# Attention and a feed-forward block woven on one core: two banks of scores per exponential, h in two PSUM banks, and statistics and output scaling shared out anew

## The chip, the cores and the metric

The kernel runs as one program on one core of one Trainium2 chip. The metric is device time in microseconds (us), the median of several executions, as the chip measures them; smaller is better.

## What is computed

Two stages, the second fed by the first. The attention stage takes q, k, v of 4 batches, 8 heads, 768 tokens and 64 features, and 16 centroids for each head. Each query and each key belongs to the centroid that it is most alike to, and a query attends only to keys of its own cluster:

```python
q_assign = np.argmax(np.einsum('bhsd,hcd->bhsc', q_n, c_n), axis=-1)   # k_assign alike
mask = q_assign[:, :, :, None] == k_assign[:, :, None, :]
scores = np.where(mask, scale * np.matmul(q, k.transpose(0, 1, 3, 2)), -1e9)
attn = softmax(scores)                       # maximum subtracted, as usual
x = np.matmul(attn, v)                       # turned to 3072 tokens of 512
h = x @ w_in                                 # 512 -> 1024
solu = h * softmax(h)
mu, var = mean(solu), mean((solu - mu) ** 2)
out = ((solu - mu) / np.sqrt(var + 1e-06) * g_ln) @ w_out     # 1024 -> 512
```

q_n, k_n and c_n are q, k and the centroids over their norms. The output is 3072 rows of 512 in float32.

## The kernel before, in words

**Order.** The kernel records each operation with a name, an engine and what it needs (the class Weave, `add`). Five tables, one for each engine (SP, POOL, PE, DVE, ACT), then say in which order that engine takes the kinds of operation: `S2 V h3` means two of the next banks of scores, one group of value products, three parts of h. A table AWAY gives single operations to another engine. The program is emitted in that order, so each engine's queue is written out by hand; waits between engines follow from the tiles.

**Attention.** The units are pairs of heads (16 in all: 4 batches by 4 pairs). For each pair, q and k are loaded (`ld`), turned by PE (`tp`, line 402, into the tile hreg), copied out (`xa`, 409; `xt` is a turn by VectorE), and multiplied by the normalised centroids (`cl`, lines 471 and 476, into a PSUM tile csc). VectorE turns the product back (`tb`), takes the maximum over centroids (`mx`), makes one-hot rows (`oh`) and turns them (`ot`); `pl` places them beside the features in the tiles qk, so that one matmul of 80 rows gives the score plus a bonus where the clusters agree. The first pair goes in halves (query or key of one head at a time), so that scores start early.

Scores (`S`, line 637) are made for 128 keys by 512 queries, one PSUM bank of 512 float32 per step: 288 banks. ScalarE takes each with one exponential (`E`, 643, tiles `e`, a ring of nine), whose scale and bias make scores without the bonus vanish. The value products (`V`, 660: six matmuls over the key tiles, 192 groups) collect six heads' outputs in one bank (ops), VectorE divides by the sum that a column of ones yields (`N`, lines 672 and 685, into x), and a DMA turns x (`tx`).

**Feed-forward.** The tokens come in 24 blocks of 128, f = 0 to 23. For each, `h` is made in four parts (746; f2 is the half of 512 columns, each half two parts of two matmuls), then: VectorE's maximum over 1024 (`hm`, 752), ScalarE's exponential with its sum (`ex`, 758, into e_sb), VectorE's product u = e * h (`u`, 765, which reads h out of PSUM a last time), a DMA transpose of u (`tu`; for the last two blocks PE does it, `ptu`, with copies out, 742), VectorE's statistics of u (`bn`, 776, two of 512; `ag`, 780) for the variance, three small steps on POOL for alpha, the factor of the row (`at`, `al`, 786 to 795), four parts of `y` (810) against the centred w_out, scaling by alpha (`sc`, 825 on ScalarE or 827 on VectorE) and the output's DMA (`ou`, 837). The work of block f lies between the scores of later units; the last three blocks end alone.

**PSUM**, eight banks: three single banks for scores (tiles sps, pool ps_s), three for h (the tile hreg), one for the value products (ps_o), one for clustering products and y (ps_m). Block f takes banks 0 and 1 of hreg where f is even, 2 and 1 where it is odd (`at` and `both`, with the halves' order changed), so one of its two halves needs only u of block f-2, and the other u of block f-1.

**Start.** The centroids are loaded (c_all), VectorE and POOL work out the inverse norm (877 to 889) and scale them (890), PE turns the result (899), VectorE masks it into blocks (903), and only then can the first clustering product run. A column sum of w_out (`su`, `me`, `ce`) centres it. Matmuls without use (`wm`, `fl`, line 854, tile idle_p) keep PE busy through the start.

Of the kernel before, what the change touches and what calls it, by code (L numbers as in the profile page):

```python
# [22 lines left out]
class Weave:  # L23
# [6 lines left out]
        ld4 lv si ld6 lv ld lg lv ld2 lo2 lv lo ld2 lo ld6 li4 tx ld lv ld6 lv tx lv tu ld5 lv ld tx  # L30
        ld tu ld tu ld8 ou ld tu ou ld4 lv ld7 lv ld tu ld4 ou tx ld tu ld4 ou tx ld5 ou ld tu ld2
        lv ld tu ld tx ld4 ou ld3 ou pl ld5 tu lv ld4 lv tu ou tu ld3 lv ou tx ld lv tu ld2 pl ou tx
        ld2 ou pl tu ou lv tx tu pl ou tu2 tx2 tu ou tx2 tu ou tu ou tx tu ou tu ou tu ou6
    """
    ORDER["POOL"] = """
        zo po =ca0.0.0.1.0 ca =pl0.0.0.1.1 pl cv =ca0.1.0.1 =ca0.1.0.0 =pl0.0.1.0.0 pl z
        =pl0.0.1.0.1 ca pl ca =cv0.1.1 =ca0.2.1.1 pl =ca0.2.0.1 pl2 ca2 =ca0.3.1.1 cv =pl0.2.0.0
        =ca0.3.1.0 cv pl =ca0.3.0.1 z pl =cv0.3.1 =ca1.0.0.0 cv =ca1.0.1.0 pl =z4 gs z ca =pl1.0.1.1
        sg ca =pl1.0.0.1 pl2 wi4 =ca1.1.1.0 =cv1.0.1 =ca1.1.0.1 cv =ca1.1.1.1 =at1 =ca1.2.0.1 at ca
        al =pl1.1.1.1 cv =pl1.1.0.0 pl bl pl ca z =ca1.2.1.1 al at ca cv =pl1.2.1.1 =pl1.2.0.0 al  # L40
        =pl1.2.0.1 pl =ca2.0.1.0 bl cv =ca1.3.0.1 at =cv1.3.1 =ca1.3.1.0 ca al =pl1.3.1.1 =pl1.3.0.0
        pl cv bl pl =cv2.1.0 ca =pl2.0.0.0 pl =at5 pl2 at al =ca2.0.1.1 =ca2.1.0.0 =pl2.1.0.1
        =ca2.1.1.1 ca cv al =ca2.3.0.0 bl cv =pl2.1.1.1 =ca2.2.0.1 =ca2.1.1.0 =pl2.1.0.0 =ca2.2.0.0
        pl bl =ca2.3.1.1 at2 al =ca2.2.1.0 cv ca cv pl =ca2.3.1.0 pl at pl =pl2.3.1.1 =pl2.3.1.0 ca
        pl at pl al =ca3.0.0.0 ca =ca3.0.1.0 bl ca =cv2.3.1 al =ca3.1.1.1 cv =pl3.0.0.0 =pl3.0.1.1
        pl bl =ca3.2.0.1 al ca =cv3.0.1 cv pl at2 ca al =pl3.1.1.1 =ca3.3.0.0 =ca3.2.0.0 =cv3.1.1
        =pl3.2.0.1 al =pl3.1.0.1 pl =ca3.2.1.0 =cv3.2.1 pl =ca3.3.0.1 cv ca cv at =ca3.3.1.0 pl cv
        al ca at =pl3.3.0.1 at =pl3.3.1.1 al pl ca =at17 at al2 at al at al =at21 at al2 =at22 at
        al3 at al
    """  # L50
    ORDER["PE"] = """
        wm fl2 tp fl2 tp fl8 cp tp fl7 cl tp fl11 cl fl16 tp S tp S cq S2 tp S tp2 S V S tp V S tp
        cl V S tp2 S V S2 V tp S V S gt tp S2 cl S2 V2 S V S tp S V S V S tp S V S cl S2 V S V3 S2
        tp2 S V S V2 S tp S V S2 cl S V S V2 S2 V S su S3 V4 S3 su S V S2 V S V2 S2 me S2 V2 S2 V2
        S2 cl S2 V S V S V2 h S3 h S h S h S V S V3 S2 h V h V S2 V S h S V S h S2 V S V h S V h S3
        V3 y2 S y S h2 S h V y S2 V2 S h cl V S2 h V h S3 h S V y S y3 V S2 V S V h V S h S V S V S
        y S h y S3 V y S V S V2 S y S V2 S2 cl h V S h S2 h V S V S2 y V S V2 S2 y S2 y2 S V h V S V
        S2 V2 S V cl S2 V2 S cl S V2 S2 y S V S V S y S V S y S V S2 y S V S V2 h V S h S h2 S y4 S
        V S h2 S V S h2 S V S V cl V h S h S V S2 cl S h S h V S2 V h S V2 h y2 S2 y2 S2 V2 S h S2 h
        V S V S2 V2 y S V2 S y S3 y h y V3 S V S2 h V S h S V h S2 h V S cl V S2 V S V cl V S2 h V  # L60
        y2 S y S V S y S2 V S V2 h S h S2 V S cl S V S2 y S y3 V2 S V S V S y S2 V y S2 V3 S2 y S y
        V2 S V2 S2 h S h S2 h2 S3 V h V S y S V S2 h V y2 S2 y V S V h S h S V3 S2 cl V h S V2 h S y
        S3 h S h S V2 y V S h y S h S y S V S2 V2 h2 S2 V2 y V y S V S h S h S2 V h2 S V y2 h2 S V2
        S2 V2 S y S2 h S2 h S V2 S V2 y S y S V S h2 S2 h S h S2 V3 S y h V S V2 h S V S h2 S2 y V S
        y S y h y S h V h2 y h V y V y S2 y S2 V h3 y4 h2 V y V y V y2 h2 ptx y4 h2 y3 h2 y ptu2 y8
        ptu2 y4
    """
    ORDER["DVE"] = """
        cn ca cf xa tb mx oh ot =pl0.0.0.0.1 pl tb xa mx xa cb cv oh xa ot xa =xa0.2.0.1 xa ca tb mx
        oh ot N gk =xa0.3.1.0 pl xa tb mx oh xa ot N tb mx cv xa N pl oh xa3 N ot =pl0.3.0.1  # L70
        =pl0.3.0.0 pl N tb mx oh ot N sk xt2 N ce2 N ce2 tb ce mx ce2 N ce hm N ca u xt bn N hm oh
        bn ag ot u N xt hm sc bn u bn2 tb hm ag mx N oh u =bn3.0 bn ot =xt1.3.1 ag bn N hm xt ag cv
        =xt2.0.1 sc N u tb mx bn oh ot xt2 cv N bn sc xt hm N tb mx oh tb N ag ot u mx xt N bn2 ag
        oh ot xt hm N xt u bn2 hm xt tb ag u mx N oh tb bn hm bn ot ag mx u oh sc N bn2 ot hm
        =xt3.0.1 N u bn xt bn N bl =xt3.1.1 xt tb ag hm mx tb oh N xt u bn sc xt ot tb hm ag N
        =mx3.2 sc =oh3.2 N u bn ag =ot3.2 N mx bn oh ot N xt sc hm ca bn ag u bn2 N xt hm bl tb bl u
        bn N ag mx hm bn cv ag oh u ot bn N hm bl u =bn15.0 bn ag hm N sc u N bn3 hm N u bn hm N u N
# [111 lines left out]
def kernel(  # L189
# [11 lines left out]
    nc = tc.nc  # L201
# [1094 lines left out]
```

## Time and profile before

| | us |
|---|---|
| median of 3 executions (226.42 to 226.63) | 226.57 |
| the profiled execution, whole | 227.3 |
| its span on the core | 225.3 |

| what the profile's page says | value |
|---|---|
| granted TensorE clock, mean | 1.00 |
| HBM read, written | 23.11 MB, 6.29 MB |
| chain that ended last, by engine | PE 80%, DVE 10% |
| the same chain, by line | scores (637) 23%, h (746) 16%, y (810) 16%, value products (660) 12% |

The page is of one profiled execution. Busy time is the sum of an engine's instructions; a busy matmul may still be drawn out by waiting. In rows that group instructions the number behind the bar is the sum of busy time, then the mean of one in ns, then the idle time ahead of them with what ended it. In rows of the chain the first number is the time from the span's start, the second the length, and a bracket names a wait. In the rows by stage the columns are named where they are shown. PEld is the loading of weights, which overlaps the matmuls. Tiles go by the program's names.

### The profile page before, as it was taken

To read this page: it belongs to the slowest core of one execution; us is meant where nothing else is said; L and a number is where in the kernel's file an instruction comes from. 1 tells how busy PE (TensorE), PEld (TensorE's weight loads), DVE (VectorE), ACT (ScalarE), POOL (GpSimd) and SP (SyncE) were. 2 spreads that over 40 slices of the span, in tenths; PEclk is the share of its full clock that TensorE was granted. 3 is DMA by queue.
4 is the path that set the end of the run, shared out by engine and by line. 5 is a ranking of instruction groups with operands and counts; after the bars stand their busy time and mean duration, and the time that the engine had idled before them with its cause. 6 is when DMAs were issued, how large, how long until landed. Compare 5 with 4: busy or idle time off the path is not lost.

```text
span 225.3 us, 6745 instructions
## 1 busy us (share of the span) xinstructions
PE 219.2 (97%) x2501; PEld 146.8 (65%) x2501; DVE 200.3 (89%) x359; ACT 191.3 (85%) x366; POOL 127.7 (57%) x246
## 2 busy tenths in 40 slices
PE   8999999999999999999999999999999999999993
PEld 8877864666666767666566656676666677665452
DVE  2799997899999999999999899898998996879982
ACT  3399988999979999998989979899989899964353
POOL 3379985942385597289995670957965102122341
PEclk9999999999999999999999999999999999999999
DMA  5999994289999999799997998789771724659522
GB/s 182 366 370 354 196 243 191 47 163 220 187 179 153 213 179 169 148 161 175 184 219 155 147 215 149 180 170 162 175 166 58 93 28 116 90 155 177 166 83 103
DMA packets 117327, 38.80 MB, mean 172 GB/s; under 512 B 105640, under 2 KB 112816, under 8 KB 117296
## 3 DMA queue, kind: packets, MB, share of 16 engines
q1 hardware_dynamic: 117008, 38.06, 79.0%
q8 instruction: 19, 0.31, 0.6%
q10 hardware_dynamic: 288, 0.33, 0.4%
q14 instruction: 12, 0.10, 0.2%
HBM read 23.11 MB, written 6.29 MB: 130 GB/s over the span
## 4 chain that ended last, share of the span: by engine, by line
PE 80%; DVE 10%; ACT 2%; POOL 2%; issue 2%; DMA 1%; SPq 1%; DVEq 0%; ACTq 0%; POOLq 0%
PE sps L637 23%; PE hreg L746 16%; PE yps L810 16%; PE ops L660 12%; PE hreg L402 3%; PE csc L476 3%; PE idle_p L854 3%; DVE xt L427 2%; ACT e L643 2%; PE csc L471 1%; DMA raw<-in_q_dram 1%; DVE nmax L752 1%; DVE y L827 1%; DVE oh L510 1%; PE hreg L609 1%
## 5 line engine op out<-in xcount | busy, mean ns | idle before, releaser
L643 ACT ACTIVATE e<-sps 128x512 bf16<-128x512 f32 x288 | 150.6, 610 | 10.5 <-PE sps L637 8.6
L637 PE MATMUL sps<-qk 80*128 80x256 bf16 (+3 forms) x648 | 98.9, 260 | 0.3
L637 PEld LDWEIGHTS <-qk 80*128 80x128 bf16 (+1 forms) x648 | 52.1, 97 | 32.0 <-issue 8.6
L660 PEld LDWEIGHTS <-e 128*128 128x128 bf16 x1152 | 52.5, 97 | 16.0 <-issue 4.0
L660 PE MATMUL ops<-v,e 128*128 128x65 bf16 x1152 | 58.7, 193 | 0.5 <-DVE x L685 0.3
L746 PE MATMUL hreg<-w_in_sb,xT 128*128 128x512 bf16 x192 | 54.4, 379 | 0.0
L810 PE MATMUL yps<-w_out_c,uT 128*128 128x512 bf16 x184 | 49.9, 379 | 0.3 <-DVE y L827 0.3
L765 DVE TENSOR_TENSOR u<-e_sb,hreg 128x1024 bf16<-128x1024 bf16 (+1 forms) x25 | 29.1, 1166 | 5.0 <-ACT e_sb L758 4.9
L758 ACT ACTIVATE e_sb<-hreg,nmax 128x1024 bf16<-128x1024 f32 x24 | 26.8, 1118 | 6.7 <-DVE nmax L752 6.5
L776 DVE BATCH_NORM_STATS2 bs<-u 128x6 f32<-128x512 bf16 x48 | 31.6, 676 | 0.3
L550 POOL COPY qk<-oht 32x384 f32<-32x384 f32 x40 | 20.6, 515 | 18.8 <-DVE oht L523 14.9
L752 DVE TENSOR_REDUCE nmax<-hreg 128x1 f32<-128x1024 f32 x24 | 28.9, 1203 | 1.3 <-PE hreg L746 1.1
L456 POOL CAST qk<-xt 64x768 bf16<-64x768 f32 (+1 forms) x31 | 25.5, 823 | 6.9 <-DVE xt L409 3.0
L458 POOL TENSOR_SCALAR qk<-xt 64x768 bf16<-64x768 f32 (+1 forms) x28 | 23.4, 836 | 4.0 <-PE yps L810 2.3
L810 PEld LDWEIGHTS <-uT 128*128 128x128 bf16 x200 | 17.8, 97 | 11.5 <-ACT uT L742 0.8
L746 PEld LDWEIGHTS <-xT 128*128 128x128 bf16 x192 | 16.5, 97 | 8.1 <-issue 0.6
L792 POOL TENSOR_SCALAR esq<-es,mv 128x1 f32<-128x1 f32 x24 | 8.1, 339 | 22.6 <-DVE mv L780 22.0
L427 DVE STREAM_TRANSPOSE xt<-raw 128x768 f32<-128x768 f32 x22 | 20.9, 959 | 0.0
L685 DVE TENSOR_TENSOR x<-ops,den 128x256 bf16<-128x256 f32 (+1 forms) x39 | 18.9, 486 | 1.3
L786 POOL TENSOR_SCALAR es<-esum 128x1 f32<-128x1 f32 x24 | 5.6, 239 | 23.3 <-ACT e_sb L758 14.9
L568 POOL CAST v<-vf 128x384 bf16<-128x384 f32 x27 | 14.3, 532 | 7.7 <-DMA vf<-in_v_dram 4.7
L795 POOL TENSOR_TENSOR alpha<-esq,halves 128x1 f32<-128x1 f32 x24 | 13.4, 560 | 2.0
(82 smaller groups left out, 186.6 us busy)
## 6 DMA issues: line engine op xcount, KB each, us to landing
vf<-in_v_dram SPq DMA_DIRECT2D x16, 384.0 KB, 4.4
out_dram<-y SPq DMA_DIRECT2D x23, 256.0 KB, 2.8
raw<-in_q_dram SPq DMA_DIRECT2D x44, 96.0 KB, 3.2
raw<-in_k_dram SPq DMA_DIRECT2D x44, 96.0 KB, 3.4
w_g<-in_moe_w_out_dram SPq DMA_DIRECT2D x4, 512.0 KB, 8.0
w_st<-in_moe_w_in_dram SPq DMA_DIRECT2D x4, 512.0 KB, 6.9
raw<-in_q_dram SPq DMA_DIRECT2D x4, 384.0 KB, 7.2
raw<-in_k_dram SPq DMA_DIRECT2D x4, 384.0 KB, 7.8
```

The lines of the kernel that those rows point to most:

```text
L427: nc.vector.transpose(xt[:], raws[b, p, i][:].rearrange("p j c -> p (j c)"))
L456: VEC[e].tensor_copy(dst, src)
L458: VEC[e].tensor_scalar(dst, src, scalar1=inv_C, scalar2=1.0, op0=Alu.mult, op1=Alu.mult)
L637: nc.tensor.matmul(sps_[n, k][:, c0:c0 + w], side(b, h // 2, 1, h % 2, keys)[r], side(b, h // 2, 0, h % 2, slice(s0 * P, s0 * P + w))[r])
L643: nc.scalar.activation(es[n, k][:, :w], sps_[n, k][:, :w], Act.Exp, scale=exp_scale, bias=-exp_scale)
L660: nc.tensor.matmul(opss[g][:, s, :VW], es[n, k][:, c0:c0 + P], v1[slot(b, h // 2)][:, h % 2, kt, :VW], start=(kt == 0), stop=(kt == n_t - 1))
L746: uses(nc.tensor.matmul(hreg[:, at(f, f2)[1], :], xTs[f][:, dc, :], w_in_sb[:, dc, f2 * FF2:(f2 + 1) * FF2], start=(dc == 0), stop=(dc == ...
L752: uses(nc.vector.tensor_reduce(ff[f, "nmax"][:], pair_of(f), axis=AXY, op=Alu.max, negate=True), *both(f))
L758: uses(nc.scalar.activation(ff[f, "e"][:], pair_of(f), Act.Exp, bias=ff[f, "nmax"][:], accum_out=ff[f, "esum"][:]), *both(f))
L765: uses(nc.vector.tensor_tensor(ff[f, "u"][:, at_], ff[f, "e"][:, at_], pair_of(f)[:, at_], op=Alu.mult), *banks)
L776: nc.vector.bn_stats(ff[f, "bs"][:, f2, :], ff[f, "u"][:, f2, :])
L810: ins = nc.tensor.matmul(dst, ff[f, "uT"][:, at(f, f2)[0] * (n_fc // 2) + c, :], w_out_c[:, fc, cols], start=(fc == chunks[0]), stop=(fc = ...
```

## The change

**Scores.** The pool of scores holds two tiles of two banks, and one exponential of 1024 elements takes both banks. Scores go into a bank when the exponential of the pair before the last is done (four banks back, where it was three). The ring of exponentials' results is five pairs of tiles.

```diff
+    RING_E = 5
-    ps_s = ctx.enter_context(tc.tile_pool(name="ps_s", bufs=3, space=bass.MemoryType.PSUM))
+    ps_s = ctx.enter_context(tc.tile_pool(name="ps_s", bufs=2, space=bass.MemoryType.PSUM))
 def scores(n, k):
-        sps_[n, k] = ps_s.tile([P, 512], F32, name="sps", tag="sps")
+        at_ = bank_at[n, k]
+        if at_ % 2 == 0:
+            sps_[at_ // 2] = ps_s.tile([P, 2, 512], F32, name="sps", tag="sps")
-    def expo(n, k):
-        es[n, k] = ep.tile([P, 512], BF16, name="e")
-        nc.scalar.activation(es[n, k][:, :w], sps_[n, k][:, :w], Act.Exp, scale=exp_scale,
-                             bias=-exp_scale)
+    def expo(j):
+        e = ep.tile([P, 2, 512], BF16, name="e")
+        pair = BANKS[2 * j:2 * j + 2]
+        for x, bank in enumerate(pair):
+            es[bank] = e[:, x]
+        m = len(pair)
+        nc.scalar.activation(e[:, :m], sps_[j][:, :m], Act.Exp, scale=exp_scale, bias=-exp_scale)
```

**h.** That leaves two banks for hreg. Both halves of a block's h now need u of the block before; block 22 takes its two banks from the pool of scores, and block 23 waits for u of block 21.

```diff
-    hreg = ps_h.tile([P, 3, FF2], F32, name="hreg")
+    hreg = ps_h.tile([P, 2, FF2], F32, name="hreg")
     def at(f, f2):
-        return (f2, f2) if f % 2 == 0 else (1 - f2, 2 - f2)
+        return (f2, f2)
     def pair_of(f):
-        return hreg[:, 0:2, :] if f % 2 == 0 else hreg[:, 1:3, :]
+        return tail["h"] if f == n_f - 2 else hreg[:]
-                    was = f - 1 if f2 else f - 2
-                    if was >= 0:
+                    was = n_f - 3 if f == n_f - 1 else f - 1
+                    if f == n_f - 2:
+                        nd.append(ename(*BANKS[2 * n_e - 4]))
+                    elif was >= 0:
                         nd.append(f"u{was}")
```

**Variance.** In 12 of 24 blocks (the odd ones up to 21, and 22) VectorE's product u also sums its row (a custom instruction, L790, and a read), a small step makes the mean (`nm`), and ScalarE sums the squares of u minus the mean (`sq`, L807, into e_sb, where the block's exponential had been). The exponential of the block after the next waits for that square. POOL's steps for alpha follow suit.

```diff
+    BY_ACT = {*range(1, n_f, 2), n_f - 2} - {n_f - 1}
     def f_u(f, half=None):
+        if f in BY_ACT:
+            h_uses(f, nc.vector.tensor_tensor_reduce(
+                out=ff[f, "u"][:], in0=ff[f, "e"][:], in1=pair_of(f), scale=1.0, scalar=0.0,
+                op0=Alu.mult, op1=Alu.add, accum_out=ff[f, "usum"]), *banks)
+            return
+    def f_mean(f, e):
+        VEC[e].tensor_scalar(ff[f, "nmean"], ff[f, "usum"], scalar1=-1.0 / d_ff, scalar2=None,
+                             op0=Alu.mult)
+
+    def f_var(f):
+        nc.scalar.activation(ff[f, "e"][:], ff[f, "u"][:], Act.Square, bias=ff[f, "nmean"],
+                             accum_out=ff[f, "usq"])
-        nd = ([f"hm{f}"] + ([f"u{f - 2}"] if f >= 2 else []) +
+        nd = ([f"hm{f}"] + ([f"{'sq' if f - 2 in BY_ACT else 'u'}{f - 2}"] if f >= 2 else []) +
```

**Outputs.** ScalarE scales all of them but one half of the last block's; before, VectorE had ten and a half. y of block 21 goes into the bank of the value products.

**Start.** The centroids are loaded twice (c_two, on two queues) and turned by PE as they come; ScalarE copies the result (`ct`). The inverse norm is worked out meanwhile, one matmul spreads it over the partitions (`ci`), and VectorE multiplies the two into the blocks, those of the first pair first (`cg`, then `cf` and `cb`). The first two loads of q go on ScalarE's queue, those of k on SP's. ScalarE takes all four first copies `xa` and one placement `pl`; 18 matmuls without use instead of 26, and 29 of the later ones instead of 46.

```diff
-    nc.vector.tensor_scalar(c_n[:], c_all[:].unsqueeze(1).to_broadcast([P, 2, D]),
-                            scalar1=c_inv[:], scalar2=None, op0=Alu.mult)
     def turn_centroids():
-        nc.tensor.transpose(cs["t"][:].rearrange("p a h c -> p (a h c)"),
-                            c_n[:].rearrange("p a d -> p (a d)"), ident_f[:])
+        cs["t"] = ps_o.tile([P, 2, P], F32, name="cps", tag="ops")
+        nc.tensor.transpose(cs["t"][:, 0, :], c_two[:].rearrange("p a d -> p (a d)"), ident_f[:])
+    def spread_inverse():
+        nc.tensor.matmul(cs["t"][:, 1, :], c_inv[:].to_broadcast([P, P]), ident_f[:])
```

**Tail.** The PE transposes of the last blocks use the two halves of one pair of banks in turn (`tail["a"]`); the copies out of them stay on the engines that had them (one of block 22 on VectorE, the other three on ScalarE, lines 740 and 742 before).

**Order.** All five tables are new. One line of PE's, with h of blocks 17 to 20 (four parts each):

```diff
+        V4 S2 h4 S2 V S2 y2 V2 S2 V S2 h4 S3 V S V3 S2 y V y V2 S h4 V S2 y4 V2 S3 y2 h4 y2 S2 V S V
```

On ScalarE before, between the exponentials of h of two blocks (e_sb out of hreg: first block 15, last block 16) stand six exponentials of one bank of scores:

```order
L758 ACTIVATE e_sb_3944,esum_3943<-hreg_111,nmax_3906 128x1024
L643 ACTIVATE e_3964<-sps_3947 128x512
L643 ACTIVATE e_3974<-sps_3956 128x512
L643 ACTIVATE e_3983<-sps_3967 128x512
L643 ACTIVATE e_3996<-sps_3978 128x512
L643 ACTIVATE e_4004<-sps_3985 128x512
L643 ACTIVATE e_4024<-sps_4009 128x512
L758 ACTIVATE e_sb_4036,esum_4035<-hreg_111,nmax_4022 128x1024
```

On ScalarE after, from the exponential of block 16 to that of block 17, the four of scores take two banks each, one of them stands right behind block 16's own, and one right ahead of block 17's; the scaling of an output is among them:

```order
L779 ACTIVATE e_sb_3617,esum_3616<-hreg_111,nmax_3584 128x1024
L649 ACTIVATE e_3640<-sps_3590 128x1024
L870 ACTIVATE y_3662<-yps_3509,alpha_3470 128x512
L649 ACTIVATE e_3676<-sps_3622 128x1024
L649 ACTIVATE e_3685<-sps_3664 128x1024
L649 ACTIVATE e_3711<-sps_3691 128x1024
L779 ACTIVATE e_sb_3731,esum_3730<-hreg_111,nmax_3698 128x1024
```

Six single banks have become four pairs, and the scaling (L870) has come between.

On VectorE at the start before, the norm of the centroids, their scaling (L890) and, behind the first placing of tokens (L458), the mask of the turned product (L903); cps is the turned product:

```order
L877 ISA c_n_148,c_nsq_149<-c_all_118 128x64
L877 ISA c_nsq_149 128x1
L882 RECIPROCAL c_r0_153<-c_s0_151 128x1
L883 SCALAR_TENSOR_TENSOR c_r0_153<-c_r0_153,c_nsq_149,c_s0_151 128x1
L886 TENSOR_SCALAR c_norm_156<-c_r0_153 128x1
L889 RECIPROCAL c_inv_158<-c_norm_156 128x1
L890 TENSOR_SCALAR c_n_148<-c_all_118,c_inv_158 128x128
L458 TENSOR_SCALAR qk0_99<-xt_211 64x3x128
L903 TENSOR_TENSOR w_out_c_113<-cps_222,own_142 128x256
L409 COPY xt_199<-hreg_111 128x384
L485 STREAM_TRANSPOSE cst_251<-csc_242 128x192
```

On VectorE at the start after, c_two is the raw centroids, c_t their turned copy, cps the spread inverse norm; L956 writes the blocks:

```order
L921 ISA c_sq_146,c_nsq_147<-c_two_118 128x64
L921 ISA c_nsq_147 128x1
L927 RECIPROCAL c_r0_151<-c_s0_149 128x1
L929 TENSOR_SCALAR c_s1_153<-c_s0_149 128x1
L931 SCALAR_TENSOR_TENSOR c_norm_155<-c_r0_151,c_nsq_147,c_s1_153 128x1
L934 RECIPROCAL c_inv_157<-c_norm_155 128x1
L956 TENSOR_TENSOR w_out_c_113<-c_t_159,cps_181 64x2x16 x2
L457 TENSOR_SCALAR qk0_99<-xt_210 64x3x128
L484 STREAM_TRANSPOSE cst_235<-csc_223 128x192
```

The scaling of the centroids is gone, the product for the first pair (L956) stands right behind the inverse norm and ahead of the tokens' step (L457), and the copy out of hreg (L409) has left VectorE.

357 lines of the change are left out of this document (193 added, 164 removed).

## The prediction

> **What bounds the kernel now.** I read the page's first part, then busy time by stage, then the chain of waits, then PE's own waits, and last the timeline at the places that the change touches.
>
> ```profile
> span 225.3 us, 6745 instructions
> PE 219.2 (97%) x2501; PEld 146.8 (65%) x2501; DVE 200.3 (89%) x359; ACT 191.3 (85%) x366; POOL 127.7 (57%) x246
> ```
>
> Three engines are nearly full, so the share of busy time doesn't decide. The stages do. The rows of h give two of their borders: block 0 starts its h at 47.2 and block 12 at 150.8 (block 21 follows at 199.2).
>
> ```profile
> L746 PE MATMUL hreg<-w_in_sb,xT x20: 377/377/382, 47.2 to 57.9; 128*128 128x512 bf16 x20
> ```
> ```profile
> L746 PE MATMUL hreg<-w_in_sb,xT x44: 377/378/383, 150.8 to 179.4; 128*128 128x512 bf16 x44
> ```
> ```profile
> 150.80:199.20 48.40, 48.30 (x570) 32.33 (x568) 42.51 (x70) 45.52 (x88) 19.69 (x40) 1.00 0.67 120
> 47.20:150.80 103.60, 102.85 (x1198) 67.97 (x1195) 98.88 (x169) 96.44 (x185) 67.32 (x122) 1.00 0.94 175
> ```
>
> The columns are length, then busy time of PE, PEld, DVE, ACT, POOL. VectorE is 95% busy in the middle and 88% later. A busy PE may still be a waiting PE, so its pace has to be read. Six adjoining steps of the chain of waits, and one clustering product:
>
> ```profile
> 91.98 0.78 PE csc L476 x8
> ...
> 187.52 0.45 PE sps L637 x8
> 187.97 0.43 PE hreg L746 x2
> 188.41 0.23 PE sps L637 x4
> 188.63 0.43 PE hreg L746 x2
> 189.07 0.45 PE sps L637 x8
> 189.52 0.55 PE ops L660 x18
> ```
>
> Each step starts where the last one ends. So this is PE's bare pace: 0.43 for a part of h (two matmuls of 512 columns, a quarter of a token block's h; y is alike), 0.22 for a bank of scores, 0.18 for a group of six value products. I multiply these by what stands in PE's order from the first scores to the last y (288 banks, 192 value groups, 96 parts of h and 96 of y, 15 full clustering products, some 11 us of transposes and column sums) and get 204. The trace takes 211, from 10.82 (below) to the end of this row:
>
> ```profile
> 220.04 1.97 PE L810 MATMUL hreg<-w_out_c,uT 128*128 128x256 bf16 x16 [0.45 <-ACT uT L742]
> ```
>
> Even if all 7 that are left were waits (part of it is small steps between kinds of work), PE is at its limit, and nothing that lightens another engine can give more than that.
>
> ```profile
> PE idle_p L854 <- DVE halves L858: 1.0, 1, 1.0
> PE hreg L810 <- ACT uT L742: 0.5, 1, 0.5
> PE ops L660 <- DVE x L685: 0.3, 1, 0.3
> PE yps L810 <- DVE y L827: 0.3, 1, 0.3
> ```
>
> PE's listed waits after the start come to about 1. So the change can gain at the start and at the tail, and a little in between; it loses wherever it makes PE wait.
>
> **The change, part by part.** *ScalarE's exponentials.* Twelve one-bank exponentials in a row, and the groups that give the other prices:
>
> ```profile
> 20.09 6.20 ACT L643 ACTIVATE e<-sps 128x512 bf16<-128x512 f32 x12
> ```
> ```profile
> L776 DVE BATCH_NORM_STATS2 bs<-u 128x6 f32<-128x512 bf16 x48 | 31.6, 676 | 0.3
> L780 DVE BATCH_NORM_AGGREGATE mv<-bs 128x2 f32<-128x12 f32 x24 | 4.6, 192 | 0.2
> L825 ACT ACTIVATE y<-yps,alpha 128x512 f32<-128x512 f32 x13 | 9.0, 692 | 5.8 <-PE yps L810 3.2 <-POOL alpha L795 2.5
> L827 DVE TENSOR_SCALAR y<-yps,alpha 128x512 f32<-128x512 f32 x10 | 7.4, 740 | 1.3 <-POOL alpha L795 0.8 <-issue 0.4
> ```
>
> 6.20 over 12 is 0.52, with the last one's end in it, which a next one would overlap: 0.51, two 1.02. No row shows a two-bank exponential of scores. The nearest is the exponential of h, with as many elements out of two banks; here are its rows with its neighbours, one token block from h to u:
>
> ```profile
> 100.56 1.03 PE L746 MATMUL hreg<-w_in_sb,xT 128*128 128x512 bf16 x4
> ...
> 101.63 1.23 DVE L752 TENSOR_REDUCE nmax<-hreg 128x1 f32<-128x1024 f32 x1
> ...
> 102.89 1.11 ACT L758 ACTIVATE e_sb<-hreg,nmax 128x1024 bf16<-128x1024 f32 x1 [0.39 <-DVE nmax L752]
> ...
> 103.90 0.19 ACT L758 ACTIVATION_READ_ACCUMULATOR e_sb<-hreg,nmax 128x1 f32 x1
> 103.99 1.07 ACT L643 ACTIVATE e<-sps 128x512 bf16<-128x512 f32 x2
> ...
> 104.21 1.18 DVE L765 TENSOR_TENSOR u<-e_sb,hreg 128x1024 bf16<-128x1024 bf16 x1
> ```
>
> From its start to the next exponential is 1.10, with the read of the sum in it: bounds 0.91 (1.10 less 0.19) and 1.02 (no gain). I take 0.92, so 144 pairs save 14.4 (0 to 16). ScalarE gets 12 squares with a sum, priced as that row (1.10): +13.2; ten scalings from VectorE at 0.69: +6.9; a few copies at the start: +1.4. It ends at 191.3 - 14.4 + 21.5 = 198, not lower. VectorE loses 24 statistics (15.8), 12 aggregates (2.3) and ten scalings (7.4), gains about 3 for the means and sums (small ones of 0.1 to 0.2): 178. By themselves both cost and gain nothing: PE's work covers them, as above. If ScalarE's cover goes, that is the third rival.
>
> *The scores' ring*: three banks become two pairs. PE's pace gives a pair 204/144 = 1.4 us, ScalarE needs 0.92 for it; with two slots, PE comes back to a slot 2.8 after it began to fill it. A pair is ready 0.65 after its start (0.22 for the first bank, 0.39 until the second is written, as in the row at 10.82 below, and a hop), so its exponential may be about 1.2 late before PE notices; with three single banks the same reckoning gives about 1.1. Priced at nothing (-1 to +2).
>
> *h in two banks.* Now a block's h may begin only after u of the block before has been read out. Before it need not:
>
> ```profile
> 174.88 0.60 PE L746 MATMUL hreg<-w_in_sb,xT 128*128 128x512 bf16 x2
> ```
> ```profile
> 175.19 1.22 DVE L765 TENSOR_TENSOR u<-e_sb,hreg 128x1024 bf16<-128x1024 bf16 x1
> ```
>
> The matmuls for block 16 start in the third bank 0.3 before u of block 15 has even begun. [...]
>
> The loop: the first four matmuls of h 0.86, then from 100.56 to u's end at 105.39 4.83, then about 0.1 to start PE again: 5.8 between the starts of two blocks, with no queue on VectorE or ScalarE. Against it stands PE's own work between those starts in the new order, from block 12 to block 21. For 17 to 18: four parts of h 1.72, eight banks 1.78, four value groups 0.73, two parts of y 0.86: 5.1. All nine: 5.95, 6.63, 5.97, 5.45, 5.46, 5.09, 5.42, 5.96, 5.92, in sum 51.9. The same count for before gives 47.45 where the trace takes 48.40, so I add 2% to each. Where scores stand between h's parts the loop grows with them: 6.0, 7.05 and 6.25 for the first three. The loop is longer than the work by 0.3, 0.2, 0.2, 0.2, 0.6 and 0.3 at six of the nine: +1.8. On top comes the queue: a two-bank exponential stands ahead of the block's own in ScalarE's order. Filled right after h, it runs from 2.4 to 3.3 of the loop, while the maximum is ready at 3.2; so 0.13 at most blocks, 0.1 for the sum that VectorE now reads with u in odd blocks, and more where a pair is late: +1.2 (0 to +3.5). So +3.0 (1.8 to 5.3).
>
> *From block 0 to block 12* the same loop meets intervals of 6 us and more; only the first four are near it. New waits about 1, old ones (some of the 1 above) gone: +0.3 (-1.5 to +3). Scalings now queue behind exponentials on ScalarE and hold the one bank of y longer; that is within the same bounds, since PE's whole wait for it was 0.3. The new order of SP moves outputs and turns among the loads; their longest cover is eight load buffers, and none of PE's waits above names a load: nothing.
>
> *Start.* What leads to the first scores now:
>
> ```profile
> 0.72 0.41 ACTq L384 DMA_DIRECT2D raw<-in_q_dram  x1
> ...
> 4.70 0.16 DVE L889 RECIPROCAL c_inv<-c_norm 128x1 f32<-128x1 f32 x1
> ...
> 4.79 0.85 PE L402 MATMUL hreg<-ident_f,raw 128*128 128x128 f32 x3
> ...
> 5.67 0.48 ACT L409 COPY xt<-hreg 128x384 f32<-128x384 f32 x1 [0.37 <-PE hreg L402]
> ...
> 6.28 0.42 PE L899 MATMUL cps<-ident_f,c_n 128*128 128x128 f32 x1
> ...
> 6.74 0.42 DVE L903 TENSOR_TENSOR w_out_c<-cps,own 128x256 f32<-128x256 f32 x1
> ...
> 7.43 0.16 PEld L471 LDWEIGHTS csc<-xt,w_out_c 128*32 128x32 f32 x8
> ...
> 10.82 0.39 PE L637 MATMUL sps<-qk 80*128 80x256 bf16 x2
> ```
>
> The clustering product at 7.43 waits for the centroids' chain (7.16), not for the tokens (6.15). After the change the raw centroids are transposed early, and the inverse norm (4.86) needs one matmul and two small products, to about 6.1: the product can start at about 6.3. That is -1.1; four placements on three engines instead of two I put at -0.2, and the first q, issued 0.45 later on ScalarE's queue, may give some back: -1.2 (-1.6 to -0.4).
>
> *Tail*: y of block 22 is left to cover the last copies of u, which cost PE 0.5 above; by hand a new wait of 0.3 for the copy on VectorE stands against it: -0.2.
>
> The sum: -1.2 + 3.0 + 0.3 - 0.2 = +1.9. The profiled execution took 227.3 (span 225.3 and 2.0 around it), the median of the runs is 226.57; the difference is carried over to the median: 228.5.
>
> **The rivals.** (1) *The loop fits*: blocks wait only where the bare loop is over the work (+1.8), and all old waits between block 0 and 12 go (-1.5), since VectorE is empty enough to take each maximum at once: 226.57 - 1.2 + 1.8 - 1.5 - 0.5 (the tail's old wait) = 225.2. For it: VectorE falls by 22. Against it: the loop's 5.8 was already taken without a queue. 0.20. (2) *PE isn't the bound, VectorE is*: then time falls with the fullest other engine, from 200 to 198, and by the start: 226.57 - 2.3 - 1.2 = 223.1. For it: 95% in the middle. Against it: the unbroken steps of PE. 0.07. [...] (3) *ScalarE becomes the bound* from block 5 on: between blocks 12 and 21 it has 33 pairs, 9 exponentials of h, 4 squares and 7 scalings, 30.4 + 9.9 + 4.4 + 4.8 = 49.5, against 45.5 before in 48.4. If each of about 30 pairs there is late by a further 0.1, it decides: 228.5 + 3 = 231.5. 0.13. (4) *No change*: start and loop cancel, 226.6. 0.08. That the change doesn't do what it says is ruled out: the order on ScalarE has the 144 exponentials of 128x1024. My forecast has 0.52, between 227.1 and 230.
>
> What a measurement of this kernel can tell from no change is about 0.2%, 0.45 us. Faster is (1) and (2) with a bit of (4): 0.28; same 0.07; slower 0.65. The range, 224.4 to 231.3, leaves out (2) and the upper part of (3).
>
> **What the new profile would show.** Right: first scores at about 9.6; 144 exponentials near 1.0 each; ScalarE at 198, VectorE at 178; h behind u by name among PE's waits, and the nine starts of h from block 12 to 21 taking 55 to 57 where their bare work takes 52.9; PE idle or stretched there, dense elsewhere. Wrong: if those nine take 53 or less, the loop is not a bound and the kernel is faster; if PE's waits name the exponentials of scores all along, it is the third rival; if the first scores stay at 10.8, the start's chain was misread.

## The result and the profile after

The changed kernel takes 232.80 us (median of 4 executions, 232.29 to 234.0), where the one before took 226.57: a ratio of 1.029 (95% interval 1.026 to 1.033; the two medians alone give 1.027). It is slower, as forecast, but by 6.2 us and not by 1.9, and above the range. The profiled execution took 232.29 whole, 5.0 more than that of before (227.3). The other 1.2 is spread between executions: that of after lies 0.5 under its median, that of before 0.7 over it.

The page's first part, after:

```profile
span 229.9 us, 6419 instructions
...
PE 218.6 (95%) x2449; PEld 145.5 (63%) x2477; DVE 181.8 (79%) x339; ACT 200.9 (87%) x259; POOL 125.9 (55%) x243
```

VectorE lost 18 us of work, ScalarE gained 10, and PE does the same in 4.6 us more of span. The chain that ended last, 80% of it on PE before, now runs through the other engines for half of the span:

```profile
PE 45%; ACT 20%; DVE 17%; POOL 8%; issue 6%; DMA 2%; ACTq 0%; DVEq 0%; POOLq 0%
```

The groups of ScalarE's exponentials and squares, and of PE's scores:

```profile
L649 ACT ACTIVATE e<-sps 128x1024 bf16<-128x1024 f32 x144 | 141.1, 1030 | 13.6 <-PE sps L640 12.9
L640 PE MATMUL sps<-qk 80*128 80x256 bf16 (+3 forms) x648 | 92.8, 260 | 3.0 <-ACT e L649 2.1
...
L807 ACT ACTIVATE e_sb<-u,bs 128x1024 bf16<-128x1024 bf16 x12 | 13.9, 1157 | 2.1 <-DVE bs L803 2.1
```

141.1 over 144 is 0.98 for a pair, nearer to two single ones (1.02) than to the 0.92 that I took. Where the time went is read by stage. Four rows of PE give the borders after the change, the first scores and the first h of blocks 0, 12 and 21 (columns: start, length):

```profile
9.53 0.60 PE L640 MATMUL sps<-qk 80*128 80x256 bf16 x4
...
48.61 0.59 PE L767 MATMUL hreg<-w_in_sb,xT 128*128 128x512 bf16 x2
...
153.11 0.81 PE L767 MATMUL hreg<-w_in_sb,xT 128*128 128x512 bf16 x3
...
208.84 0.81 PE L767 MATMUL hreg<-w_in_sb,xT 128*128 128x512 bf16 x3
```

Busy time of the engines between these borders, after (columns as in the prediction: stretch, length, then PE, PEld, DVE, ACT, POOL):

```profile
9.53:48.61 39.08, 36.94 (x470) 26.38 (x471) 35.99 (x72) 33.10 (x37) 28.41 (x48) 1.00 0.88 227
48.61:153.11 104.50, 103.07 (x1180) 68.15 (x1195) 89.85 (x159) 98.60 (x124) 68.45 (x124) 1.00 0.99 176
153.11:208.84 55.73, 53.33 (x616) 35.55 (x623) 39.61 (x69) 51.70 (x69) 20.48 (x45) 1.00 0.57 115
208.84:229.90 21.06, 17.41 (x116) 9.02 (x114) 11.95 (x22) 12.62 (x21) 4.99 (x13) 0.98 0.50 129
```

The two stretches of before that the prediction did not show:

```profile
10.82:47.20 36.38, 35.86 (x472) 25.71 (x472) 33.49 (x69) 33.60 (x67) 28.99 (x47) 1.00 0.80 234
...
199.20:225.30 26.10, 22.32 (x167) 12.10 (x165) 19.83 (x35) 11.92 (x21) 8.02 (x21) 1.00 0.50 130
```

The new order puts other work into a stretch, so from each length I take PE's own work in it, counted with the prediction's prices:

| stretch | length before, after | PE's work before, after | lost by the change | forecast |
|---|---|---|---|---|
| to the first scores | 10.82, 9.53 | | -1.3 | -1.2 |
| to h of block 0 | 36.38, 39.08 | 34.4, 34.3 | +2.8 | 0 |
| to h of block 12 | 103.60, 104.50 | 100.0, 100.3 | +0.6 | +0.3 |
| to h of block 21 | 48.40, 55.73 | 47.45, 51.9 | +2.9 | +3.0 |
| to the end | 26.10, 21.06 | 22.6, 17.6 | 0.0 | -0.2 |

The last column's terms hold but for one: the stretch of 39 us behind the first scores loses 2.8, twice what the start gained. PE's listed waits, after:

```profile
PE sps L640 <- ACT e L649: 2.1, 6, 0.7
...
PE hreg L401 <- DMA raw<-in_q_dram: 0.7, 1, 0.7
PE ops L665 <- DVE x L690: 0.5, 2, 0.3
PE hreg L401 <- DVE xt L408: 0.5, 2, 0.3
...
PE hreg L767 <- DVE bs L803: 0.2, 1, 0.2
```

They name exponentials of scores. The first matmul of h is named only once, behind the small step for the mean (L803) that follows u on VectorE. One loop shows why (ScalarE, VectorE and PE, from h of block 17 to h of block 18):

```profile
185.02 1.89 PE L767 MATMUL hreg<-w_in_sb,xT 128*128 128x512 bf16 x8
...
186.95 1.23 DVE L773 TENSOR_REDUCE nmax<-hreg 128x1 f32<-128x1024 f32 x1 [0.94 <-PE hreg L767]
...
188.38 1.11 ACT L779 ACTIVATE e_sb<-hreg,nmax 128x1024 bf16<-128x1024 f32 x1
...
189.47 2.85 ACT L649 ACTIVATE e<-sps 128x1024 bf16<-128x1024 f32 x3
...
189.71 1.22 DVE L790 CUSTOM_DVE_ANT_0 u<-e_sb,hreg 128x1024 bf16<-128x1024 bf16 x1 [0.93 <-issue]
190.55 0.61 PE L640 MATMUL sps<-qk 80*128 80x128 bf16 x8 [0.68 <-ACT e L649]
...
191.00 1.90 PE L767 MATMUL hreg<-w_in_sb,xT 128*128 128x512 bf16 x8
```

h, maximum, exponential, u and the next h follow each other with gaps of 0.2 or less, 5.98 in all. But the exponential of scores that starts at 189.47 ends at 190.5 too, and frees the pair that PE fills just ahead of h. From the block's exponential two paths lead to the next h, and they end within 0.1 of each other.

### The profile page after: what moved, and what is told of

Same layout as the page of the kernel before. It is cut to its first block, busy times and chain, and to the rows that moved or that the text cites. A ratio compares the mean times of both kernels' runs of the same rounds, so it can differ in the third digit from the quotient of the medians.

```text
span 229.9 us, 6419 instructions
## 1 busy us (share of the span) xinstructions
PE 218.6 (95%) x2449; PEld 145.5 (63%) x2477; DVE 181.8 (79%) x339; ACT 200.9 (87%) x259; POOL 125.9 (55%) x243
## 4 chain that ended last, share of the span: by engine, by line
PE 45%; ACT 20%; DVE 17%; POOL 8%; issue 6%; DMA 2%; ACTq 0%; DVEq 0%; POOLq 0%
ACT e L649 13%; PE sps L640 13%; PE hreg L767 11%; PE yps L855 10%; PE ops L665 5%; ACT e_sb L779 4%; ACT e_sb L807 2%; DVE xt L408 2%; POOL qk L457 2%; POOL qk L455 2%; DVE u L790 2%; DVE cst L484 2%; DVE nmax L773 2%; DMA raw<-in_q_dram 2%; PE hreg L401 1%
## 5 line engine op out<-in xcount | busy, mean ns | idle before, releaser
L649 ACT ACTIVATE e<-sps 128x1024 bf16<-128x1024 f32 x144 | 141.1, 1030 | 13.6 <-PE sps L640 12.9
L640 PE MATMUL sps<-qk 80*128 80x256 bf16 (+3 forms) x648 | 92.8, 260 | 3.0 <-ACT e L649 2.1
L665 PE MATMUL ops<-v,e 128*128 128x65 bf16 x1152 | 56.5, 193 | 1.0 <-DVE x L690 0.5
L855 PE MATMUL yps<-w_out_c,uT 128*128 128x512 bf16 x163 | 45.6, 379 | 1.2 <-DVE uT L759 0.3
L767 PE MATMUL hreg<-w_in_sb,xT 128*128 128x512 bf16 x177 | 45.3, 379 | 0.6 <-DVE bs L803 0.2
L455 POOL CAST qk<-xt 64x768 bf16<-64x768 f32 (+1 forms) x31 | 25.8, 832 | 9.6 <-DVE xt L426 3.4
L855 PEld LDWEIGHTS <-uT 128*128 128x128 bf16 x200 | 17.4, 97 | 11.3 <-ACT uT L761 0.6
L457 POOL TENSOR_SCALAR qk<-xt 64x768 bf16<-64x768 f32 (+1 forms) x28 | 23.0, 822 | 1.2
L837 POOL TENSOR_SCALAR esq<-es,mv 128x1 f32<-128x1 f32 x12 | 4.1, 339 | 26.7 <-DVE mv L817 22.7
L870 ACT ACTIVATE y<-yps,alpha 128x512 f32<-128x512 f32 x23 | 16.0, 694 | 2.8 <-POOL alpha L840 1.7
L794 DVE TENSOR_TENSOR u<-e_sb,hreg 128x1024 bf16<-128x1024 bf16 (+1 forms) x13 | 14.8, 1138 | 3.6 <-ACT e_sb L779 3.2
L790 DVE CUSTOM_DVE_ANT_0 u<-e_sb,hreg 128x1024 bf16<-128x1024 bf16 x11 | 13.4, 1219 | 4.3 <-ACT e_sb L779 3.1
L813 DVE BATCH_NORM_STATS2 bs<-u 128x6 f32<-128x512 bf16 x24 | 16.2, 683 | 0.2
```

The costliest lines, as they stand in the source:

```text
L455: VEC[e].tensor_copy(dst, src)
L457: VEC[e].tensor_scalar(dst, src, scalar1=inv_C, scalar2=1.0, op0=Alu.mult, op1=Alu.mult)
L640: nc.tensor.matmul(sps_[at_ // 2][:, at_ % 2, c0:c0 + w], side(b, h // 2, 1, h % 2, keys)[r], side(b, h // 2, 0, h % 2, slice(s0 * P, s0 * ...
L649: nc.scalar.activation(e[:, :m], sps_[j][:, :m], Act.Exp, scale=exp_scale, bias=-exp_scale)
L665: nc.tensor.matmul(opss[g][:, s, :VW], es[n, k][:, c0:c0 + P], v1[slot(b, h // 2)][:, h % 2, kt, :VW], start=(kt == 0), stop=(kt == n_t - 1))
L767: h_uses(f, nc.tensor.matmul(pair_of(f)[:, f2, :], xTs[f][:, dc, :], w_in_sb[:, dc, f2 * FF2:(f2 + 1) * FF2], start=(dc == 0), stop=(dc == ...
```

## The experiments

Times are medians; ratios are to runs of the kernel before on the same chip. "Loop" is the time from one block's first h to the next one's.

**Is it u's hold on h's banks?** The product is made without h, in all blocks but the last:

```diff
+        other = ff[f, "e"][:] if f < n_f - 1 else pair_of(f)
-                out=ff[f, "u"][:], in0=ff[f, "e"][:], in1=pair_of(f), scale=1.0, scalar=0.0,
+                out=ff[f, "u"][:], in0=ff[f, "e"][:], in1=other, scale=1.0, scalar=0.0,
```

> The changed kernel (232.8), but u is made from e_sb alone (e times e, except in the last block), so that h's two banks come free when the exponential of h has read them, not when u has. The factor h is left out of u; all other work and every queue stays. Gate theory (each block's h waits for u of the block before, and that loop of 5.9 to 6.0 is the bound): the loop loses u's 1.2 and its hop, the nine starts of h from block 12 to 21 fall from 55.9 to 52 to 53.5 us, the others in loops of about 6 to 7 lose a little too; 227.5 to 229.5 in all. Rival, ScalarE is the bound: it has the same work, so 232 to 233. Rival, the scores' two pairs make PE wait: 232 to 233 as well.

Measured: 236.51, ratio 1.044 (1.042 to 1.047), slower yet. Its first scores came at 11.30 (more on that below), 1.8 later than in the profile above, and its first h 1.8 later. Another 2.8 went between blocks 0 and 12, where one wait is long, for GpSimd's placing of tokens:

```profile
PE sps L640 <- POOL qk L457: 1.4, 1, 1.4
```

GpSimd's two groups of such placings (L455, L457) took 917 and 910 ns each in this run, where they took 832 and 822 (more in the last section), so the whole time doesn't answer the question. The nine starts do: they took 55.37, against 55.73, so releasing h alone gains next to nothing. In its trace (from block 16's exponential to h of block 17) u is done at 188.6, and h still waits for the two banks of scores ahead of it:

```profile
186.68 1.11 ACT L779 ACTIVATE e_sb<-hreg,nmax 128x1024 bf16<-128x1024 f32 x1
...
187.77 1.02 ACT L649 ACTIVATE e<-sps 128x1024 bf16<-128x1024 f32 x1
187.91 0.69 DVE L795 TENSOR_TENSOR u<-e_sb 128x1024 bf16<-128x1024 bf16 x1 [0.34 <-ACT e_sb L779]
...
188.84 0.61 PE L640 MATMUL sps<-qk 80*128 80x128 bf16 x8 [0.24 <-ACT e L649]
...
189.29 1.89 PE L767 MATMUL hreg<-w_in_sb,xT 128*128 128x512 bf16 x8
```

**Is it ScalarE's amount of work?** Once less, once more:

```diff
-        nc.scalar.activation(ff[f, "e"][:], ff[f, "u"][:], Act.Square, bias=ff[f, "nmean"],
+        nc.scalar.activation(ff[f, "e"][:, 0, :8], ff[f, "u"][:, 0, :8], Act.Square, bias=ff[f, "nmean"],
```

> The changed kernel (232.8), but ScalarE's sum of squares goes over 8 elements a row, not 1024, so that the variance of twelve blocks is wrong. ScalarE loses about 10 us of work (12 x 0.85), of which 3.4 between blocks 12 and 21. Gate theory: the loops have no square on their path, only sometimes ahead of it in ScalarE's queue: 0 to -1, so 231.8 to 232.8. Rival, ScalarE is the bound from block 0 on: the time falls with its work, by 6 to 9, to 224 to 227, and the nine starts take 52.5 where they took 55.9.

```diff
-        nc.scalar.activation(e[:, :m], sps_[j][:, :m], Act.Exp, scale=exp_scale, bias=-exp_scale)
+        for x in range(m):
+            nc.scalar.activation(e[:, x], sps_[j][:, x], Act.Exp, scale=exp_scale, bias=-exp_scale)
```

> The changed kernel (232.8), but each pair of banks of scores is read by two exponentials of 512, one behind the other, into the same tile. ScalarE gains about 9.5 us of work (150.6 busy before against 141.1), 2 of them between blocks 12 and 21, and the first of the two may begin before the second bank is written. Gate theory: each block's own exponential stands behind a slightly longer one, +0.1 on the loop at most, and the gaps elsewhere take the rest: 232.5 to 235. Rival, ScalarE is the bound: +7 to +10, 240 to 243. Rival, the pair's late start is what PE waits for: faster, 230 to 232.

Measured: with the small square 233.15 (1.031, 1.028 to 1.033), no gain in the median (its trace is 0.5 shorter, 0.4 of it ahead of block 12), though ScalarE is busy for 9 us less:

```profile
PE 218.1 (95%) x2449; PEld 145.6 (63%) x2477; DVE 181.7 (79%) x339; ACT 191.7 (84%) x259; POOL 126.0 (55%) x243
```

Its nine starts took 55.72, the same to 0.01. So the amount of ScalarE's work is not the bound. With single exponentials 236.88 (1.047, 1.044 to 1.050); its first h was 2.1 late, and from there to the last matmul it took 181.5 against 178.1. The 3.4 lie between the two theories: 2.6 of them between blocks 0 and 12 and 0.9 in the nine loops, while PE's listed waits for exponentials of scores rose from 2.1 to 3.8:

```profile
PE sps L640 <- ACT e L650: 3.8, 11, 0.8
```

That fits a path that leads through ScalarE's queue, where a longer exponential of scores costs though a shorter square saves nothing.

**Cut both paths.** For blocks 16 to 18, h goes ahead of the scores that it stood behind, and the block's exponential ahead of the pair's:

```diff
-  S V4 y S2 h4 S3 V y V S2 y S   V4 S2 h4 S2 V S2 y2 V2 S2 V S2 h4 S3
+  S V4 y h4 S5 V y V S2 y S   V4 h4 S4 V S2 y2 V2 S2 V h4 S5
-  E3 sq E ex E sc E3 ex E4 ex E sc
+  E3 sq ex E2 sc E2 ex E4 ex E2 sc
```

In the first and the third of three kernels u is also made from a constant in float32, without h:

```diff
+            one = ident_f[:].unsqueeze(1).to_broadcast([P, d_ff // P, P])
+            nc.vector.tensor_tensor(u_, e_, one, op=Alu.mult)
```

> The changed kernel (232.8), with two edits together. u is made from e_sb and a constant in float32 (the factor h left out), so that h's banks come free behind the exponential; and for blocks 16, 17 and 18 h stands ahead of the two banks of scores that it stood behind on PE, and the block's exponential ahead of the pair's on ScalarE. Theory (the loop of 5.9 has two equal paths behind each block's exponential: u's read of h, and the exponential of scores that frees the pair which PE fills ahead of the next h; that is why releasing h alone gained nothing): with both cut, the loops from 16 to 17 and 17 to 18 fall from 5.9 and 6.0 to 5.1 to 5.5, the others stay at 5.9 to 6.1. Rival (the loop is PE's or ScalarE's own work): they stay at 5.9. In all within 1.5 of 232.8, the late start aside.

> The changed kernel (232.8) with the sum of squares over 8 elements (variance of twelve blocks wrong; the square alone changed nothing), and with h of blocks 16, 17 and 18 ahead of the two banks of scores that it stood behind on PE, the block's exponential ahead of the last pair's on ScalarE. h's banks still wait for u. Theory (two equal paths lead from a block's exponential to the next h, u's read of h and the pair's exponential that PE's scores ahead of h wait for): only one is cut, so the loops from 15 to 18 stay at 5.8 to 6.1. Rival (the pair's exponential alone is the bound, u would have been in time): they fall to 5.1 to 5.5.

> As the run before (square over 8 elements, h of blocks 16 to 18 ahead), and u made from e_sb and a constant, so that h's banks are free behind the exponential (the factor h is left out of u). Theory (two equal paths, both cut now): the loops 15 to 16, 16 to 17 and 17 to 18 fall to 5.0 to 5.5, where each was 5.9 to 6.0 with either path left. Rival (the loop is the engines' own work, or ScalarE's): 5.8 to 6.1.

In the second and the third ScalarE squares only 8 elements a row, as above. Measured: 243.35 (median of 4), and 236.24 and 239.02 (one execution each). The reordering itself does harm: the loops 16 to 17 and 17 to 18 rose to 7.4 and 6.2 in the last two runs alike. In the second run ScalarE idles 1.94 for the scores that were put off behind block 16, and PE then waits 2.3 in all for the exponentials. These two loops say nothing on the question. (In the first run the granted clock fell to 0.76 from 186 to 200, so what comes later in it is not read.) The loop from 15 to 16 lies ahead of the harm. First h of blocks 15 and 16, in the changed kernel, with u released, with h ahead, and with both:

```profile
173.24 0.61 PE L767 MATMUL hreg<-w_in_sb,xT 128*128 128x512 bf16 x2 [0.20 <-DVE bs L803]
...
179.12 0.60 PE L767 MATMUL hreg<-w_in_sb,xT 128*128 128x512 bf16 x2
```
```profile
177.51 0.60 PE L767 MATMUL hreg<-w_in_sb,xT 128*128 128x512 bf16 x2
...
183.38 0.60 PE L767 MATMUL hreg<-w_in_sb,xT 128*128 128x512 bf16 x2
```
```profile
174.54 0.60 PE L767 MATMUL hreg<-w_in_sb,xT 128*128 128x512 bf16 x2 [0.21 <-DVE bs L803]
...
180.33 0.60 PE L767 MATMUL hreg<-w_in_sb,xT 128*128 128x512 bf16 x2 [0.46 <-DVE bs L790]
```
```profile
177.97 0.60 PE L767 MATMUL hreg<-w_in_sb,xT 128*128 128x512 bf16 x2
...
183.12 0.59 PE L767 MATMUL hreg<-w_in_sb,xT 128*128 128x512 bf16 x2
```

5.88, 5.87, 5.79 and 5.15 (and 5.15 in the first run, which has both, with the whole square). These lengths don't hold the same work: with h ahead, the two banks of scores that stood between the two h, 0.45 of PE's time, stand behind the second. For equal work the first two are 5.43 and 5.42, the others 5.79 and 5.15. So releasing u alone gains nothing, putting h ahead alone loses 0.36 (PE waits 0.46 for u's row, by the bracket, where it had two banks to fill), and both together gain 0.28. PE's own work for 5.15, by the prediction's prices, is 5.0. Either path alone holds the loop. It is one loop of nine, seen in two runs.

**The banks as before, under the new orders.** Three single banks of scores and three of hreg, with `at` and `both` as before:

```diff
-        sps_[at_ // 2] = ps_s.tile([P, 2, 512], F32, name="sps", tag="sps")
-    hreg = ps_h.tile([P, 2, FF2], F32, name="hreg")
+        sps_[n, k] = ps_s.tile([P, 512], F32, name="sps", tag="sps")
+    hreg = ps_h.tile([P, 3, FF2], F32, name="hreg")
```

> The changed kernel (232.8), with the banks as before: three single banks of scores, three of hreg used in turn by h and by the tokens, and so an exponential for each bank of scores; the new orders, the squares, the scalings and the new start stay (in the tail, the maximum of block 23 goes behind u of block 22). ScalarE has the 9.5 us of work more that cost 3.4 of PE's time in the changed kernel with single exponentials, beside a late start there. Theory (the time is lost to the loop of h and to the scores' two pairs, not to ScalarE's squares or scalings): the nine starts from block 12 to 21 fall from 55.9 to 50 to 53, and 228 to 231 in all, far under the 236.9 of two single exponentials. Rival (ScalarE's work is the bound): 235 to 238.

Measured: 253.64 (1.120, 1.116 to 1.124), far over both expectations. PE's first wait:

```profile
PE sps L638 <- ACT e L648: 16.2, 24, 1.5
```

The new order of PE counts on four banks of scores; with three it stops at ScalarE in nearly every loop. What the banks are worth can't be read under an order that was made for others.

**The start.** First all of the new start on the kernel before, of which this is PE's order, then, on the changed kernel, q's load first on its queue, then more idle matmuls:

```diff
-    wm fl2 tp fl2 tp fl8 cp tp fl7 cl tp fl11 cl fl16 tp S tp S cq S2
+    wm fl2 cp fl6 tp2 ci tp fl cl tp fl8 cl fl12 tp S tp S3
```

> The kernel before (226.57), with the change's start alone: raw centroids loaded twice and turned early, the inverse norm spread by a matmul, q's first loads on ScalarE's queue, the first four copies and one placement on ScalarE, fewer idle matmuls; everything else, the three banks and its orders, as before. The prediction's step (the start's gain is kept): first scores at 9.5 to 9.7 instead of 10.8, and 225.2 to 225.6 in all. Rival (the stretch from the first scores to the first h is set by VectorE, 92% busy there, which does the same work): first scores as early, h of block 0 still at 47 to 47.4, and 226.3 to 226.8 in all.

```diff
+    load_head(0, 0, 0, 0, nc.scalar)
     nc.scalar.dma_start(out=c_two[:, 1, :], in_=centroids.rearrange("h c d -> (h c) d"))
-    load_head(0, 0, 0, 0, nc.scalar)
```

> The changed kernel (232.8), with one issue moved: ScalarE's queue issues the first load of q ahead of its copy of the centroids, as before the change, so that it is out at 0.7 and not at 1.2. Theory (the start is lost to the late q: in four runs PE idles 0.7 to 1.8 us for that load, and in three of them its first clustering products are slower afterwards, first scores at 11.3 to 11.9): the first tokens are turned at 3.9 to 4.3, first scores at 9.0 to 9.5 in every run, and the time falls by 0.5 to 1.5 with a smaller spread, to 231.3 to 232.3. Rival (the start of the scores doesn't matter, VectorE sets the stretch behind it): first scores earlier, h of block 0 still near 48.6, and 232.8.

```diff
-        wm fl2 cp fl6 tp2 ci
+        wm fl2 cp fl12 tp2 ci
```

> The changed kernel (232.8), with twelve idle matmuls instead of six between the transpose of the centroids and the first of the tokens, so that PE stays busy while it waits for q. Theory (what varies from run to run at the start is a gap on PE: after 0.65 us of it the six transposes of the tokens took 0.88 together and first scores came at 9.5; after 0.7 to 1.0 in other kernels they took 1.5, and scores came at 10.9 to 11.4; after 1.8 the granted clock was 0.5 from 7.6 to 10.5): first scores at 9.5 to 9.9, transposes at 0.14 to 0.16 each, and 231.6 to 232.4 with less spread. Rival (the late load alone makes the difference): first scores 9.5 to 11 by how late q lands, and 232.8.

Measured: 227.85 (1.007, 1.004 to 1.009), 234.13 (1.034, 1.031 to 1.038) and 232.69 (1.029, 1.027 to 1.031). Alone, the new start loses 1.5 and gains nothing. In all three q's first tokens were turned later than the 3.93 of before; the first scores came at 11.36, 10.93 and 9.92, where they came at 10.82 before and at 9.53 in the changed kernel. In the start alone the stretch from there to h of block 0 is longer too, 37.75 against 36.38, though its three banks are those of before; PE waits 0.9 in it for VectorE's copy of tokens. The first tokens' transposes and first scores of the start alone:

```profile
4.87 1.54 PE L402 MATMUL hreg<-ident_f,raw 128*128 128x128 f32 x6 [0.73 <-DMA raw<-in_q_dram]
...
11.36 0.38 PE L639 MATMUL sps<-qk 80*128 80x256 bf16 x2
```

With q first, the centroids landed later (2.3 and 2.9 after their issues, where the changed kernel has 1.7 and 1.9; turned at 4.25 and not at 3.08), and PE's order, which has them ahead of the tokens, waited for those (tokens at 5.13, scores at 10.93). With the filled start the time did not change. Nine of the kernels here have the new start as it stands in the changed kernel, with one trace each. In three the first scores came at 9.5 to 9.6, the changed kernel among them; in six they came at 11.3 to 11.9, later than before the change. Five of the six have slow first transposes (1.54 for six, where the three have 0.88), and the sixth turned its first tokens only at 5.92 and then ran at a granted clock of 0.57 for 4 us (last section). So the gain of 1.3 is there in some runs only; what the other executions of the changed kernel did, no trace shows.

**Two banks for the tokens' transposes.** On the kernel before, h untouched:

```diff
-                tps[b, p, i, hf] = len(ring_h) % 3
+                tps[b, p, i, hf] = len(ring_h) % 2
```

> The kernel before (226.57), but the tokens of the first pairs are turned through two of hreg's three banks, not three, as in the changed kernel; h keeps its three. If these two banks are what makes the changed kernel lose 2.7 us between the first scores and the first h, most of it shows here: 228 to 229.3, with h of block 0 at 48.5 to 50. If the new order and the scores' pairs make it, 226.3 to 227.2.

Measured: 228.04 (1.007, 1.005 to 1.009); h of block 0 at 49.27, 2.1 late; the stretch from the first scores took 38.76, 2.4 more than before. PE's waits from 9.4 to 50.5:

```profile
PE hreg L402 <- DVE xt L409: 2.1, 3, 0.9
PE hreg L402 <- ACT xt L409: 0.6, 1, 0.6
```

Each transpose now waits for the copy of the one before the last.

**VectorE's pace.** In the changed kernel, with the filled start, two of those copies and a cast of v go to ScalarE:

```diff
-  DVE  cn cg ca tb mx oh ot pl2 cv tb xa mx cf xa2 cb xa oh
+  DVE  cn cg ca tb mx oh ot pl2 tb xa mx cf xa cb oh
-  ACT  pl E2 =ca0.0.1.0.1 ca E2
+  ACT  pl cv E xa E xa =ca0.0.1.0.1 ca E2
```

> The changed kernel with the filled start (12 idle matmuls, 232.7), and three pieces of VectorE's work behind the first scores given to ScalarE, which waits 5.3 us for scores in that stretch: two copies of tokens out of hreg (0.54 each) and the first cast of v (0.68). Theory (in the changed kernel the 39 us from the first scores to h of block 0, 36.4 before, are what VectorE lets through: it is 92% busy there, and 1.2 of PE's 1.7 named waits are for its copies of tokens, its division and its cast): those waits fall by half or more, the stretch falls from 38.9 by 0.8 to 2, and 231 to 232 in all. Rival (the order of PE and the two banks for tokens set the stretch, whoever copies): it stays at 38.5 to 39.1, and 232.4 to 233.

Measured: 231.41 (1.024, 1.021 to 1.026), 1.3 under the filled start (1.029). Scores at 10.29, h of block 0 at 48.02: the stretch fell from 38.9 to 37.7, and the waits for the tokens' copies are gone.

**Both lessons on the kernel before.** Raw centroids turned early but behind the first tokens, q first, 26 idle matmuls, later blocks multiplied on GpSimd:

```diff
+    wm fl8 tp2 cp ci fl2 tp fl cl tp fl8 cl fl12 tp S tp S3
+    add("cf", "POOL", 0.6, -490, lambda e: keep_blocks(c_by_two[:, 2:H], 2, H, 1, nc.gpsimd), ["cu", "ct"])
```

> The kernel before (226.57) with a start made from both: q's first load ahead of everything on ScalarE's queue as before, raw centroids turned early as in the change but behind the first tokens on PE, 26 idle matmuls in all ahead of the tokens as before, and the blocks for later pairs multiplied by GpSimd from a copy, so that VectorE has only the first pair's. All else as before. If the start's chain is what I took it for, first scores at 9.2 to 9.9, no slow matmuls, and 225.2 to 226.0, faster than both. Rival (VectorE's or the loads' pace behind the first scores sets h of block 0): first scores as early, h of block 0 at 47.2 or later, 226.4 to 227.2.

Measured: 225.65 against 226.10 beside it (0.9981, 0.9957 to 1.0004). Scores at 10.02 and h of block 0 at 46.32, both 0.8 to 0.9 early: the gain of a start does reach h when nothing behind it gets slower. It is under the change by 3%, and too near to the kernel before to be called faster.

## Why the prediction was wrong, point by point

- **The bound.** Right: PE does the same work, and what makes it wait is what costs. Rival 2, with the fullest other engine, would have had the time fall.
- **The step that failed: the start**, -1.2 in the sum. Its first half held in the profile (scores at 9.53), with some luck: six of nine kernels with this start have them at 11.3 or later. And I let the gain pass to the end as if the next 39 us could not change, and took h as all that two banks of hreg touch. The tokens of the first five pairs are turned through hreg as well, and I had not priced that. On the kernel before, two banks for them cost 2.1 up to block 0 and 1.6 in all. The new start with three banks lengthens the same stretch by 1.4. In the changed kernel 1.2 of the 2.8 came back when VectorE had less to do there. How the 2.8 divide between banks, VectorE and order stays open: the listed waits there add up to 1.7, 0.5 of them for the tokens' copies, the rest for divisions, casts and exponentials. q's late load, which I named ("may give some back") and put at 0.1 in the sum, turned the first tokens 0.8 to 2.0 later than before.
- **h in two banks**, +3.0: right in size and place (nine starts in 55.73, forecast 55 to 57), and only half right in mechanism. The loop of 5.8 to 6.0 is held by u and, no less, by the scores' two pairs behind ScalarE's queue. That second path I had priced at nothing, as a matter of averages: a pair every 1.4 us, 0.92 to empty it. In the loops shown it binds where the block's exponential stands ahead in the queue. That the size came out is luck in part: the path that I left out ends at the same moment as the one that I counted. The nine loops took 55.73 for 51.9 of work, but giving h's banks back earlier, alone, gained only 0.4 in all nine (55.37).
- **Rival 3**, as a matter of ScalarE's total, is refuted by the small square. The sign that I had given for it, PE's waits naming the exponentials of scores, was a bad one: they name them, and less work on ScalarE still gains nothing. What is true in it is that single pairs come late.
- **The small terms** (blocks 0 to 12, the tail) came within 0.3. ScalarE (200.9 for 198) and VectorE (181.8 for 178) were near; a pair takes 0.98, so the change's central saving was 6 (9.5 by the busy sums, 150.6 to 141.1), not 14, and it did not shorten the path.

## What to carry to other kernels

When a buffer loses a bank, list all that pass through it, the start's small work too, and price each. When a wait is removed and nothing happens, look for a second path that ends at the same moment; only cutting both shows either, and the work moved by the cut has to be taken off before lengths are compared. And a gain at the start reaches the end only if nothing behind it gets slower.

## What the runs showed of the hardware

- *TensorE's speed in the first microseconds varied between the runs.* Six transposes took 0.88 in one kernel and 1.54 in another with the same start, at a shown clock of 1.00 (4.70 and 4.87 in their traces). In the run with single exponentials PE idled 1.8 for q, and then:

```profile
7.00:11.00 4.00, 3.98 (x34) 2.35 (x34) 3.15 (x9) 2.47 (x6) 1.39 (x4) 0.57 1.05 377
```

A granted clock of 0.57 for 4 us. What set it, no run here shows. My own account, that a gap of 0.7 to 1.0 decides, did not hold: six transposes took 0.88 behind a gap of 0.78 (small square) and 1.54 behind one of 0.62 (banks as before), and the kernel before and the mended start have slow first transposes without any gap (three in 0.85, six in 1.49).
- *A product of VectorE with both inputs in SBUF varied in length* (u from e_sb): the plain one took 0.69 to 1.30, the one that also sums 1.22 to 1.68, where nearly all of both take 1.22 with h out of PSUM. GpSimd's busy time in that run was 137.1, where it was 125.9 in the changed kernel. Whether the product caused that, no run here separates.
